# Sliding-window attention and a gated feed-forward block: half 1's attention early in tile 0, tile 0's outputs in tile 1, longer bursts of attention work

## The chip, the core and the metric

The kernel runs on one core of a Trainium2 chip. The core has a matrix engine (TensorE, in the profile PE, with PEld for its weight loads), a vector engine (DVE), a scalar engine (ACT), GpSimd (POOL) and a sync engine (SP) that here only starts transfers. PE writes to PSUM, eight banks of 128 x 512 fp32; DVE and ACT read them. The metric is the time of one execution on the device in microseconds; the median over several runs is compared.

## What is computed

```python
def _attn_ref(q, k, v, n_global, n_local):            # q, k, v: 4 x 8 x 768 x 64
    scores = scale * np.matmul(q, k.transpose(0, 1, 3, 2))
    is_global = pos[None, :] < int(n_global)          # 8
    is_local = (rel >= 0) & (rel < int(n_local))      # 96
    dist = np.where(is_global & ~is_local, float(n_local), np.abs(rel))
    scores = scores - slopes[:, None, None] * dist
    scores = np.where(is_global | is_local, scores, -1e9)
    a = softmax(scores)
    return np.matmul(a, v)

def _moe_ref(x, w_gate, w_val, w_out):                # x: 3072 x 512, ff 1536
    g = x @ w_gate
    return (g * sigmoid(g) * (x @ w_val)) @ w_out
```

The attention's result, heads side by side, is the x of the feed-forward block: 4 batches of 768 tokens, 8 heads of 64, a hidden width of 1536.

## The kernel before

**Tiles.** The 3072 tokens are eight tiles of 384, two to a batch ("half 0" and "half 1" of it). Tile t needs `xT`, the attention's result for its half, transposed, as four chunks of 128 features. Its feed-forward runs over twelve blocks f of 128 hidden units: four matmuls give the gate product (`gps`), four the value product (`vps`), each into one PSUM bank. ACT makes a tanh of the gate (`th`, L513), DVE turns it into x times sigmoid (`sl`, L515) and multiplies the value product by it (`hT`, L519). The banks of these products rotate over x0, x1, x2. An output is 128 tokens by 512; its twelve matmuls come in four parts of three (`out_part`, bank o0), three outputs to a tile; ACT evicts an output after its fourth part and SP stores it.

**Attention.** Heads go in pairs (`Pair`), two pairs to a quad (`Quad`). A pair's scores are taken for seven chunks of keys in three banks' worth of queries, called bk 0, 1 and 2; each head of a pair has a bank of its own out of a0 to a3 (`bank`, `banks`). ACT takes the exponential into `at`; DVE or POOL multiplies by masks that hold the bias and the window. `Quad.values` weighs: a denominator (matmuls with ones) and two numerators into PSUM, ACT copies the numerators (`ns`), DVE inverts the denominator (`invert`) and spreads it over the lanes (`spread`), and two multiplies by `scale_num` give two chunks of `xT`. These are on DVE for batch 0 and on POOL for the others.

**Batches.** Batch 0 is done in a head: half 0 completely before the first feed-forward block, with its bias put in by matmuls (`bias`). Its half 1 (`half1`: `trh` transposes, `sch` scores, `va` values) runs among the blocks of tile 0. Batch 1 is transposed by PE in tile 1 (`first`); batches 2 and 3 are loaded as rows by POOL and transposed by DMA from SP's queue (`fetch`, `transposes_dma`, `turn_ends`) inside the double tiles 2-3 and 4-5 (`both`); `second` is what is left of batch 3, in tile 6.

**Order.** All engines run their instructions in the order in which the program issues them. Six stretches of tiles each have a list of attention steps; a quota, worked out from the sum of work, hands out a step after so many products or output parts (L733 to L760). What follows a burst on ACT and DVE (exponentials of a second pair, masks, inversion, spread, multiplies) goes into a list `later`, of which one item is issued ahead of each product or output part (`run_later(1)`), and all before a further step. Loads have places of their own (`at_step`, L719 to L731), as have the masks (L716 to L718).

**Loads.** POOL starts the loads of q, k, v and the weights, which change fp32 to fp16 on the way (L594 to L612): the weights in pieces of two blocks (`load_w`), half 1 of batch 0 by `load_half(1, ...)`, v in chunks of 120 keys (`load_v_rest`), the output weights by `load_wo`. SP copies the eight global keys and values to their places and stores outputs.

Of the kernel before, what the change touches and what calls it, by code (L numbers as in the profile page):

```python
# [9 lines left out]
FP32 = mybir.dt.float32  # L10
# [6 lines left out]
WIN = 216  # L17
# [20 lines left out]
def kernel(  # L38
# [117 lines left out]
    def stage_rows(b):  # L156
        qst[b] = sb2.tile([128, NP, J, 2, D], FP16, name="qst", tag="qst")
        kst[b] = sb2.tile([128, NP, J, 2, D], FP16, name="kst", tag="kst")
        kend[b] = sb2.tile([128, H, D], FP16, name="kend", tag="kend", bufs=1)
        nc.gpsimd.memset(kend[b], 0.0)  # L160
        nc.sync.dma_start(out=kend[b][0:NG], in_=kG[:, b])
        for hp in range(NP):
            pair = kG[:, b, 2 * hp:2 * hp + 2, :].rearrange("p h d -> p (h d)")
            nc.sync.dma_start(
                out=kst[b][0:NG, hp].rearrange("p t e d -> p t (e d)"),
                in_=pair.unsqueeze(1).broadcast_to([NG, J, 2 * D]))
# [9 lines left out]
    kG = sb.tile([NG, B, H, D], FP16, name="kG")  # L176

    def load_globals():
        for dst, src in ((kG, k), (vG, v)):
            nc.gpsimd.dma_start(  # L180
                out=dst[:, 1:].rearrange("p b h d -> p (b h) d"),
                in_=src[1:, :, 0:NG, :].rearrange("b h p d -> p (b h) d"))
# [55 lines left out]
    def banks(name, dt=FP32):  # L238
        return [bank(name, dt) for _ in range(2)]

# [15 lines left out]
    class Pair:  # L256
# [97 lines left out]
        def scores(self, bk, mul_eng, put_off):  # L354
            hp = self.hp
            sc = banks("sc")
# [45 lines left out]
    class Quad:  # L402
# [33 lines left out]
        def invert(self, den):  # L436
            dT = sb2.tile([128, TB], FP32, name="dT", tag="dT")
            self.dR = sb2.tile([128, TB // 32], FP32, name="dR", tag="dR")
            nc.vector.transpose(dT, den[:, 0:TB])  # L439
            nc.vector.reciprocal(  # L440
                out=self.dR, in_=dT.rearrange("p (n i) -> p n i", i=32)[:, :, 0])
# [10 lines left out]
        def values(self, half, bank, mul_eng):  # L452
# [3 lines left out]
            for side in range(2):  # L456
                num = bank("num")
                self.weigh(half, num, side)
                src = sb2.tile([128, TB], FP32, name="ns", tag="ns")
                nc.scalar.copy(out=src, in_=num[:, 0:TB])  # L460
                srcs.append(src)
# [25 lines left out]

    hTs = {}
# [3 lines left out]
    def products(t, f, which, c0, c1, dst=None):  # L492
        if f == 0 and which == 0 and c0 == 0:
            hTs[t] = sb2.tile([128, NFF, TB], FP16, name="hT", tag="hT", bufs=3)
        if c0 == 0:
            if dst is None:
                dst = single("gv"[which] + "ps", state["x"][gv.get("n", 0) % len(state["x"])])
                gv["n"] = gv.get("n", 0) + 1
            gv[f, which] = dst
# [94 lines left out]
    load_w(0, 2)  # L594
    load_w(2, 4)
    load_w(4, 6)
    load_half(1, 0, 4)
    load_half(1, 4, 8)
    load_w(6, 8)
    load_w(8, 10)  # L600
    for c in range(3, NCH):
        load_v_rest(0, c)
    load_w(10, 12)
    for g in range(3):
        load_wo(g)
    stage(1)
    load_qk(1, 0, 4)
    load_wo(3)
    load_qk(1, 4, 8)
    load_globals()  # L610
# [30 lines left out]
    def sc(b, hp, bk):  # L641
        on_vector = b < 2 or bk < 2 or hp % 2 == 0
        return lambda: pairs[b, hp].scores(bk, nc.vector if on_vector else nc.gpsimd, bool(later))

    def va(b, g, half):
        return lambda: quads[b, g].values(half, bank, nc.vector if b == 0 else nc.gpsimd)
# [4 lines left out]
    def trh(hp):  # L651
        def step():
            pairs[0, hp].transposes_half(1, [t[:, 0:TB] for t in banks("trs", FP16)], V, A)
        return step
# [9 lines left out]
    def second(b):  # L664
        return [[sc(b, 0, 2), sc(b, 1, 2)], [sc(b, 2, 2), sc(b, 3, 2)],
                [va(b, 0, 1)], [va(b, 1, 1)]]

    def fetch(b, *hps):
        def step():
            if hps[0] == 0:  # L670
                turn_ends(b)
            for hp in hps:
                pairs[b, hp].transposes_dma()
        return step

    def first(b):
        return [[tr(b, 0), tr(b, 1)], [sc(b, 0, 0), sc(b, 0, 1)], [tr(b, 2), tr(b, 3)],
                [sc(b, 1, 0), sc(b, 1, 1)], [sc(b, 2, 0), sc(b, 2, 1)], [va(b, 0, 0)],
                [sc(b, 3, 0), sc(b, 3, 1)], [], [va(b, 1, 0)]]

    def both(b):

        n = b + 1

        return [[sc(b, 0, 2), sc(b, 1, 2)], [sc(b, 2, 2), sc(b, 3, 2), fetch(n, 0, 1)],
                [va(b, 0, 1)], [va(b, 1, 1)],
                [sc(n, 0, 0), sc(n, 0, 1), fetch(n, 2, 3)], [sc(n, 1, 0), sc(n, 1, 1)],
                [va(n, 0, 0)], [sc(n, 2, 0), sc(n, 2, 1)],
                [sc(n, 3, 0), sc(n, 3, 1)], [va(n, 1, 0)]]

    half1 = [[trh(0), trh(1)], [trh(2), trh(3)], [sch(0)], [sch(1)],
             [va(0, 0, 1)], [sch(2)], [sch(3)], [va(0, 1, 1)]]

    def ff(t, f0, f1, n_out=(0,)):
# [3 lines left out]
        (ff(0, 0, 4), [], 0, 0),  # L700
        (ff(0, 4, 11) + [(0, 11, 3)], half1, 4.7, 0.4),
        (ff(1, 0, 12, (0, 1, 1, 1)), first(1), 5.0, 0.2),
        (ff(2, 0, 12, (1,)) + ff(3, 0, 12, (1,)), both(1), 6.0, 0.4),
        (ff(4, 0, 12, (1,)) + ff(5, 0, 12, (1,)), both(2), 6.0, 0.4),
        (ff(6, 0, 12, (1,)), second(3), 6.0, 0.4),
        (ff(7, 0, 12, (1,)), [], 0, 0)]

# [8 lines left out]
    for h in range(H):  # L716
        mask_at(0, min(h, 11) if h < 4 else 11, h // 4, h, WIN, 3 * WIN)
        mask_at(h // 4, (8, -4)[h // 4] + h, 0, h, 0, WIN)  # L718
    at_step(1, 1, lambda: [copy_globals(b) for b in range(1, B)])  # L719
    for b, base, rate, v_at in ((2, 19, 2.0, (27, 28, 29, 30, 32, 33, 34)), (3, 43, 1.4, (54, 55, 56, 57, 61, 62, 63))):  # L720
# [13 lines left out]
    for tiles, steps, tail, owed in stretches:  # L734
        groups = []
        for t, f, n_out in tiles:
            groups += [(1.0, t, f, which) for which in range(2)]
            groups += [(1.1, t, f, 2)] * n_out
        work = sum(g[0] for g in groups)
        quota = len(steps) / (work - tail)  # L740
        for w, t, f, which in groups:
            if which == 0:
                for ld in loads.pop((t, f), []):
                    ld()
                if f == 0:
                    run_later(len(later))
            run_later(1)
            if which == 2:
                out_part(*outs.pop(0))
            else:  # L750
                gate_or_val(t, f, which, NC if t == 0 and f < 2 else 0)
                for fn in after.pop((t, f, which), []):
                    fn()
            owed += w * quota
            while owed >= 1.0 and steps:
                run_later(len(later))
                for step in steps.pop(0):
                    step()
                owed -= 1.0
        assert not steps  # L760
# [40 lines left out]
```

The softmax here doesn't subtract the row's maximum and nothing guards it: scores larger than these inputs give would overflow.

## Time and profile before

| | |
|---|---|
| median of 13 runs | 249.35 us (248.46 to 251.6) |
| the profiled execution | 250.95 us, its span 249.2 us |
| PE idle over the span (span less busy) | 9.6 us |
| gate and value products, `gps` and `vps` (L502), 752 matmuls | 77.9 and 77.3 us busy |
| output parts (L531), 276 matmuls | 73.1 us busy |
| DVE `sl` and `hT` (L515, L519), 94 each | 52.0 and 51.9 us busy |
| ACT `th` (L513), 94 | 46.4 us busy |
| ACT exponentials (L373), 72 | 33.2 us busy |
| POOL `xT` multiplies (L464), 24 | 23.9 us busy, 1013 ns each |
| DVE `xT` multiplies (L464), 4 | 2.0 us busy, 548 ns each |
| loads by POOL, rate of all transfers in the first 56 us | 143 to 204 GB/s |

Busy times overlap: PE's matmuls are pipelined, and an entry begins before the one ahead of it has ended. So the distance between starts is the measure of what a matmul costs in a row of others. The idle column of a row of the profile is time of that engine alone; it costs something where the engine is the one that everything waits for.

### The profile page before, as it was taken

Reading aid. Unit: us, or ns where it says so; the run is one execution under the profiler, and the core shown is the slowest. Engines: PE = TensorE matmul, PEld = TensorE weight load, DVE = VectorE, ACT = ScalarE, POOL = GpSimd, SP = SyncE. Lnnn points to the kernel's source line nnn. Section 1 sums busy time; section 2 is a strip of 40 time slices with the busy share of each in tenths; the row PEclk is TensorE's granted clock in tenths of the full one; section 3 lists DMA queues with packets and bytes.
Section 4 is the critical chain, followed back from the end, with each engine's and each line's share of the span. In section 5 each row is a group of like instructions: output and inputs, shape, how many; then the busy total and the mean of one; then the engine's idle time right before and its main releaser. Section 6 shows DMA issues by size and latency. Waiting matters only on the chain.

```text
span 249.2 us, 6076 instructions
## 1 busy us (share of the span) xinstructions
PE 239.6 (96%) x2428; PEld 135.5 (54%) x2428; DVE 159.6 (64%) x346; ACT 130.1 (52%) x289; POOL 116.2 (47%) x139
## 2 busy tenths in 40 slices
PE   6998979999998999999999999999999999999994
PEld 4555545566564555555555555555555555555543
DVE  5668636578885666767775666676766666555510
ACT  5636656787762564564743744555635634332321
POOL 8899986461099934505519777703030232200000
PEclk9999988999999999999999999999999999999999
DMA  8999999999149999941917999951011101100122
GB/s 143 167 171 181 185 173 199 204 162 139 43 36 139 119 159 142 142 73 45 93 45 86 83 158 171 177 74 43 3 42 45 42 3 42 42 10 35 42 85 87
DMA packets 86644, 25.10 MB, mean 101 GB/s; under 512 B 72800, under 2 KB 83672, under 8 KB 86616
## 3 DMA queue, kind: packets, MB, share of 16 engines
q0 software_dynamic: 67472, 14.05, 65.7%
q1 hardware_dynamic: 18584, 10.30, 18.1%
q8 instruction: 19, 0.31, 0.5%
q10 hardware_dynamic: 560, 0.36, 0.5%
q14 instruction: 9, 0.07, 0.1%
HBM read 28.67 MB, written 6.29 MB: 140 GB/s over the span
## 4 chain that ended last, share of the span: by engine, by line
PE 76%; POOL 4%; ACT 1%; issue 1%; DVE 0%; POOLq 0%
PE ops L531 23%; PE gps L502 22%; PE vps L502 21%; PE sc L365 3%; PE num L429 3%; PE den L429 2%; POOL xT L464 1%; POOL qst L193 1%; PE trs L267 1%; PE ops L547 1%; POOL kst L193 1%; ACT at L348 0%; POOL kend L198 0%; DVE sl L515 0%; ACT th L513 0%
## 5 line engine op out<-in xcount | busy, mean ns | idle before, releaser
L515 DVE SCALAR_TENSOR_TENSOR sl<-th,gps 128x384 f32<-128x384 f32 x94 | 52.0, 553 | 52.0 <-ACT th L513 51.3
L513 ACT ACTIVATE th<-gps 128x384 f32<-128x384 f32 x94 | 46.4, 494 | 67.1 <-PE gps L502 65.4
L502 PE MATMUL gps<-xT,wg 128*128 128x384 f16 x376 | 77.9, 328 | 1.3 <-POOL xT L464 1.1
L502 PE MATMUL vps<-xT,wv 128*128 128x384 f16 x376 | 77.3, 328 | 0.7 <-DVE sl L515 0.7
L531 PE MATMUL ops<-wo,hT 128*128 128x512 f16 x276 | 73.1, 379 | 0.0
L519 DVE TENSOR_TENSOR hT<-vps,sl 128x384 f16<-128x384 f32 x94 | 51.9, 552 | 12.1 <-PE vps L502 4.7
L464 POOL TENSOR_TENSOR xT<-ns,rb 128x384 f16<-128x384 f32 x24 | 23.9, 1013 | 72.5 <-DVE rb L445 72.5
L502 PEld LDWEIGHTS <-wg 128*128 128x128 f16 x384 | 36.5, 98 | 33.7 <-issue 2.4
L502 PEld LDWEIGHTS <-wv 128*128 128x128 f16 x384 | 36.3, 98 | 27.2 <-issue 3.6
L531 PEld LDWEIGHTS <-hT 128*128 128x128 f16 x276 | 26.2, 98 | 23.5 <-issue 0.4
L373 ACT ACTIVATE at<-sc 128x432 f16<-128x432 f32 x72 | 33.2, 534 | 9.6 <-PE sc L365 9.6
L170 POOL DMA_DIRECT2D vS<-in_v_dram x28 | 24.8, 899 | 6.5 <-DMA wo<-in_moe_w_out_dram 2.3
L537 ACT ACTIVATE osb<-ops 128x512 f32<-128x512 f32 x23 | 13.7, 597 | 16.7 <-PE ops L531 16.7
L460 ACT COPY ns<-num 128x384 f32<-128x384 f32 x28 | 12.0, 482 | 10.5 <-PE num L429 9.6
L384 DVE TENSOR_TENSOR at<-at,masks 128x864 f16<-128x864 f16 x20 | 12.1, 607 | 7.0 <-ACT at L373 7.0
L193 POOL DMA_DIRECT2D kst<-in_k_dram x16 | 14.1, 889 | 0.0
L429 PE MATMUL num<-at,vS 128*32 128x216 f16 (+6 forms) x560 | 12.3, 226 | 1.7 <-DMA vS<-in_v_dram 1.7
L193 POOL DMA_DIRECT2D qst<-in_q_dram x16 | 13.7, 868 | 0.0
L348 ACT ACTIVATE at<-sc 128x432 f16<-128x432 f32 (+2 forms) x32 | 11.6, 446 | 3.7 <-PE sc L340 3.7
L384 POOL TENSOR_TENSOR at<-at,masks 128x864 f16<-128x864 f16 x4 | 7.3, 1820 | 13.3 <-ACT at L373 13.3
L429 PEld LDWEIGHTS <-vS 128*32 128x32 f16 x560 | 9.7, 95 | 2.3 <-DMA vS<-in_v_dram 2.1
L439 DVE STREAM_TRANSPOSE dT<-den 128x384 f32<-128x384 f32 x16 | 9.3, 578 | 1.6 <-PE den L429 1.6
(71 smaller groups left out, 175.1 us busy)
## 6 DMA issues: line engine op xcount, KB each, us to landing
out_dram<-osb SPq DMA_DIRECT2D x23, 256.0 KB
vS<-in_v_dram POOLq DMA_DIRECT2D x24, 120.0 KB, 6.4
wg<-in_moe_w_gate_dram POOLq DMA_DIRECT2D x12, 128.0 KB, 5.4
wv<-in_moe_w_val_dram POOLq DMA_DIRECT2D x12, 128.0 KB, 5.3
wo<-in_moe_w_out_dram POOLq DMA_DIRECT2D x4, 384.0 KB, 8.6
qst<-in_q_dram POOLq DMA_DIRECT2D x16, 96.0 KB, 3.7
kst<-in_k_dram POOLq DMA_DIRECT2D x16, 90.0 KB, 3.8
kst<-in_k_dram POOLq DMA_DIRECT2D x2, 384.0 KB, 11.2
```

Source lines behind the costliest of these rows:

```text
L170: nc.gpsimd.dma_start(out=vSs[b][NG:NG + n, c, :, :], in_=v[b, :, KC * c:KC * c + n, :].rearrange("h p d -> p h d"))
L193: nc.gpsimd.dma_start(out=st[b][p0:p0 + n, h // 2, :, h % 2, :], in_=src[b, h, 0:n * J].rearrange("(t p) d -> p t d", p=n))
L373: nc.scalar.activation(out=at[:, hi, :], in_=sc[hi][:, 0:BANK], func=AF.Exp, scale=scale)
L384: mul_eng.tensor_mul(at, at, m[:, :, o:o + BANK])
L429: nc.tensor.matmul(dst[r, o:o + n], lhsT=ones[:, 0:32] if side is None else vals[:, 4 * g + j, side::2], rhs=pairs[b, 2 * g + j // 2].at[c ...
L464: mul_eng.tensor_mul(self.x_out(half, side), srcs[side], self.rb)
L502: nc.tensor.matmul(gv[f, which][:, 0:TB], lhsT=w[:, c, 128 * f:128 * f + 128], rhs=x_of(t)[:, c, :], start=(c == 0), stop=(c == NC - 1))
L513: nc.scalar.activation(out=th, in_=dst[:, 0:TB], func=AF.Tanh, scale=0.5)
L515: nc.vector.scalar_tensor_tensor(out=sl, in0=th, scalar=1.0, in1=dst[:, 0:TB], op0=AluOp.add, op1=AluOp.mult)
L519: nc.vector.tensor_mul(hTs[t][:, f, :], dst[:, 0:TB], gv["sl"])
L531: nc.tensor.matmul(ops, lhsT=hTs[t][:, f, 128 * i:128 * i + 128], rhs=wo[:, f, :], start=(f == 0), stop=(f == NFF - 1))
L537: nc.scalar.mul(out=osb, in_=ops, mul=0.5)
```

## The change

It does seven things.

1. Half 1 of batch 0 is loaded between the first weights: heads 0 to 3 after blocks 0 and 1, heads 4 to 7 after blocks 2 and 3. The rest of v comes ahead of the weights of blocks 8 to 11, the global keys and values ahead of the last output weights.
2. `half1` gets written-out places, at the end of blocks 1 to 9 of tile 0; two of its transposes share one bank each.
3. No output part is left in tile 0. Tile 1 has all twelve, five of them in its last block, and the last values of batch 1's half 0 stand between the first and the second of these five.
4. The quota is gone: every step has a tile and a block after which, or an output part before which, it is issued. A step of scores takes two or three pairs; with three, the first of them takes two banks of the rotation x0 to x2 (`spare`).
5. In tiles 2 to 6 both quads of a half are weighed in one step (`both_values`): two denominators into `spare` banks with their inversions at once, then four numerators into a0 to a3. The first quad's multiplies stay on POOL, the second's go to DVE. Batch 1's half 0 is multiplied on DVE too.
6. In the double tiles pairs 0 and 1 of the next batch are scored at block 5 of the first tile, together with the last pair of the batch before; `turn_ends` comes behind the transposes of pairs 2 and 3.
7. Buffers and smaller places: `dT` one buffer, `ns` four; `kG` without the unused batch 0; the masks from block 7 of tile 0 to block 4 of tile 1; `copy_globals` at block 7 of tile 1; loads of batch 2 from block 20 (counted over all tiles), of batch 3 from block 38.

```diff
-    kG = sb.tile([NG, B, H, D], FP16, name="kG")
+    kG = sb.tile([NG, B - 1, H, D], FP16, name="kG")
...
+    def spare(name):
+        tag = state["x"][gv.get("n", 0) % len(state["x"])]
+        gv["n"] = gv.get("n", 0) + 1
+        return single(name, tag)
...
+    def both_values(b, half):
+        two = [quads[b, g] for g in range(2)]
+        for quad in two:
+            den = spare("den")
+            quad.weigh(half, den, None)
+            quad.invert(den)
+        srcs = {}
+        for g, quad in enumerate(two):
+            for side in range(2):
+                num = bank("num")
+                quad.weigh(half, num, side)
+                src = sb2.tile([128, TB], FP32, name="ns", tag="ns", bufs=4)
+                nc.scalar.copy(out=src, in_=num[:, 0:TB])
+                srcs[g, side] = src
...
+        def spread_first():
+            two[0].spread()
+            for side in range(2):
+                scale_num(nc.gpsimd, 0, side)
+
+        later.append(spread_first)
+        later.append(two[1].spread)
+        for side in range(2):
+            later.append(lambda side=side: scale_num(nc.vector, 1, side))
...
     load_w(0, 2)
+    load_half(1, 0, 4)
     load_w(2, 4)
+    load_half(1, 4, 8)
     load_w(4, 6)
-    load_half(1, 0, 4)
-    load_half(1, 4, 8)
     load_w(6, 8)
-    load_w(8, 10)
     for c in range(3, NCH):
         load_v_rest(0, c)
+    load_w(8, 10)
     load_w(10, 12)
-    for g in range(3):
-        load_wo(g)
+    load_wo(0)
+    load_wo(1)
     stage(1)
     load_qk(1, 0, 4)
+    load_globals()
+    load_wo(2)
     load_wo(3)
     load_qk(1, 4, 8)
-    load_globals()
...
+    def sc(b, *units):
+        def step():
+            for i, (hp, bk, *other) in enumerate(units):
+                pair = pairs[b + 1 if other else b, hp]
+                on_vector = pair.b < 2 or bk < 2 or hp % 2 == 0
+                pair.scores(bk, nc.vector if on_vector else nc.gpsimd, bool(later),
+                            [spare("sc") for _ in range(2)] if len(units) == 3 and i == 0
+                            else banks("sc"))
+        return step
...
-        return lambda: quads[b, g].values(half, bank, nc.vector if b == 0 else nc.gpsimd)
+        return lambda: quads[b, g].values(half, bank, nc.vector if b < 2 else nc.gpsimd)
...
     def fetch(b, *hps):
         def step():
-            if hps[0] == 0:
-                turn_ends(b)
             for hp in hps:
                 pairs[b, hp].transposes_dma()
+            if hps[0] > 0:
+                turn_ends(b)
         return step
...
+    def first(t, b):
+        return {(t, 3): [tr(b, 0), tr(b, 1)],
+                (t, 5): [sc(b, (0, 0), (0, 1), (1, 0))],
+                (t, 7): [tr(b, 2), tr(b, 3)],
+                (t, 8): [sc(b, (1, 1), (2, 0), (2, 1))],
+                (t, 9): [va(b, 0, 0)],
+                (t, 10): [sc(b, (3, 0), (3, 1))],
+                (t, 11, 1): [va(b, 1, 0)]}
+
+    def both(t, b):
 
         n = b + 1
...
+        return {(t, 0): [sc(b, (0, 2), (1, 2), (2, 2)), fetch(n, 0, 1)],
+                (t, 5): [sc(b, (3, 2), (0, 0, n), (1, 0, n)), fetch(n, 2, 3)],
+                (t, 8): [vas(b, 1)],
+                (t + 1, 0): [sc(n, (0, 1), (1, 1), (2, 0))],
+                (t + 1, 4): [sc(n, (2, 1), (3, 0), (3, 1))],
+                (t + 1, 8): [vas(n, 0)]}
+
+    def second(t, b):
+        return {(t, 0): [sc(b, (0, 2), (1, 2))], (t, 3): [sc(b, (2, 2), (3, 2))],
+                (t, 7): [vas(b, 1)]}
+
+    half1 = {(0, 1): [trh(0, "o0"), trh(1)], (0, 2): [sch(0)], (0, 3): [sch(1), trh(2), trh(3)],
+             (0, 5): [sch(2)], (0, 6): [va(0, 0, 1)], (0, 7): [sch(3)], (0, 9): [va(0, 1, 1)]}
...
     stretches = [
-        (ff(0, 0, 4), [], 0, 0),
-        (ff(0, 4, 11) + [(0, 11, 3)], half1, 4.7, 0.4),
-        (ff(1, 0, 12, (0, 1, 1, 1)), first(1), 5.0, 0.2),
...
+        (ff(0, 0, 12), half1),
+        (ff(1, 0, 6, (0, 0, 0, 1, 0, 1)) + ff(1, 6, 11, (1,)) + [(1, 11, 5)], first(1, 1)),
...
+    spots = [(0, f) for f in (7, 8, 9, 10, 11, 11)] + [(1, f // 2) for f in range(10)]
+    for n, (t, f) in enumerate(spots):
+        mask_at(t, f, n % 2, n // 2, *((0, WIN), (WIN, 3 * WIN))[n % 2])
+    at_step(1, 7, lambda: [copy_globals(b) for b in range(1, B)])
+    for b, base, rate, v_at in ((2, 20, 2.0, (31, 32, 33, 34, 35, 36, 37)), (3, 38, 1.4, (56, 57, 58, 59, 60, 61, 62))):
...
+    def take(step_list):
+        run_later(len(later))
+        for step in step_list:
+            step()
...
+            for which in range(2):
+                run_later(1)
                 gate_or_val(t, f, which, NC if t == 0 and f < 2 else 0)
...
+            for n in range(n_out):
+                if (t, f, n) in steps:
+                    take(steps.pop((t, f, n)))
+                run_later(1)
+                out_part(*outs.pop(0))
+            if (t, f) in steps:
+                take(steps.pop((t, f)))
```

## The prediction

> **What bounds the kernel now.** I read the engine shares first, then TensorE's waits, then the stretches, then the order of time. TensorE (PE) is busy 96% of the span, so two things can be won: the other 4%, and PE time that is busy without doing dense products.
>
> ```profile
> PE 239.6 (96%) x2428; PEld 135.5 (54%) x2428; DVE 159.6 (64%) x346; ACT 130.1 (52%) x289; POOL 116.2 (47%) x139
> ...
> PEclk9999988999999999999999999999999999999999
> ```
>
> ```profile
> PE num L429 <- DMA vS<-in_v_dram: 1.7, 2, 1.4
> ...
> PE gps L502 <- POOL xT L464: 1.1, 2, 0.6
> ```
>
> ```profile
> 31.20:37.40 6.20, 4.46 (x83) 2.49 (x78) 2.25 (x5) 3.14 (x8) 5.22 (x8) 0.88 1.59 173
> 37.40:43.60 6.20, 6.20 (x60) 3.34 (x58) 3.95 (x8) 4.29 (x12) 3.73 (x6) 0.84 1.25 199
> ...
> 46.10:77.20 31.10, 31.09 (x358) 17.87 (x356) 25.09 (x54) 21.88 (x52) 15.05 (x19) 1.00 1.11 108
> ```
>
> The second fence is PE's waits (us in total, times, longest), the third its stretches: PE, weight load, DVE, ACT and POOL busy us, then PE's clock and the DMA share. The losses sit in tile 0 (about 18.5 to 48 us) and at the start of tile 2 (77 to 79 us). In tile 0 PE waits 1.42 + 0.32 us for values of batch 0, and right after that its clock is halved (the two 8s; 0.88 and 0.84). In tile 1 (third stretch row) PE is full, but DVE is at 25.09 of 31.10 us, which matters below.
>
> From tile 2 on PE streams without a gap, and only its order costs:
>
> ```profile
> 62.27 0.81 PE L531 MATMUL ops<-wo,hT 128*128 128x512 f16 x3
> 63.01 0.54 PE L365 MATMUL sc<-qT,kT 64*128 64x216 f16 x8
> 63.49 0.82 PE L502 MATMUL gps<-xT,wg 128*128 128x384 f16 x4
> ...
> 77.24 0.49 PE L502 MATMUL gps<-xT,wg 128*128 128x384 f16 x2
> 78.16 0.32 PE L502 MATMUL gps<-xT,wg 128*128 128x384 f16 x1 [0.43 <-POOL xT L464]
> 79.10 0.32 PE L502 MATMUL gps<-xT,wg 128*128 128x384 f16 x1 [0.62 <-POOL xT L464]
> 79.26 0.81 PE L502 MATMUL vps<-xT,wv 128*128 128x384 f16 x4
> ```
>
> Starts are what count: a gate or value product (four matmuls) and an output part (three) each take 0.65 us from start to start elsewhere. From the output part at 62.27 to the gate at 63.49 is 1.22 us, so the score burst between costs 0.57 us. Its two pairs stream 2 x 432 columns; at the dense rate (384 columns in 0.1625 us) that is 0.37 us. So **0.21 us of each burst is the changeover** into half-array matmuls and back.
>
> **Part 1: tile 0.** Counting starts from 18.51 us (the first gate not woven into the head), tile 0 holds ten blocks of 1.30 us, four bursts of biased scores of 1.10, two of values of 1.03, and transposes of about 1.5; with 0.1 us of changeover for each of seven bursts that is 21.7 us. Now it ends, less its nine output parts (1.95 us), at 46.3 us: 27.8 us. The 6 us lost are the waits listed for PE there (0.65 + 0.32 + 0.22 + 0.32 + 1.42 + 0.17 = 3.1), 1.65 from the halved clock (four matmuls at 35.98 take 1.25 instead of 0.65, the next four 1.28, the burst at 38.51 1.51 instead of 1.10), and some 1.2 in bank waits inside the transposes.
>
> The new order of loads. POOL's queue lands in order; from the trace's landings a weight piece takes 0.67 us, a half-head piece of k or q 1.03, a chunk of v about 0.95. Weights of blocks 0 and 1 land at 15.1 as now. Then, summing: half 1 heads 0-3 at 17.1, weights 2-3 at 19.8 (now 17.8), heads 4-7 at 22.0, weights 4-5 at 25 (now 21.4), 6-7 at 28, v at 32.6 (now 35.5), weights 8-9 at 35 (now 31), 10-11 at 37.7 as now. In the new order PE wants weights 2-3 at 19.5, 4-5 at 26.5, v at 32, 8-9 at 35.6, 10-11 at 39.5: the moved weights cost nothing, v some 0.2 us. The halved clock goes with the 1.4 us wait.
>
> What is late next is **PSUM banks and DVE**. Walking it: the first scores at block 2 take the bank of the transposes just before, whose six copies on DVE (1.27 us, behind the products of blocks 0 and 1, which end at 20.7) finish at 22.0: 0.55 us. The second transposes wait for exponentials in their bank: 0.3. Delayed gates after bursts (a pair's four exponentials take 1.5 us and hold up the next tanh): 0.6. And the last values are at block 9, two blocks (2.6 us) before tile 1, since the nine output parts that lay between are gone. From the start of that burst to the last xT multiply took 5.5 us before (43.19 to 48.67); one more gate product on DVE (0.55) comes between; PE needs it after 1.13 + 2.6 + 0.49 = 4.2: a **new wait of about 1.6 us at tile 1's start**. Behind it all of tile 1 is queued. Sum: 18.5 + 21.7 + 3.3 = 43.5 against 46.3, **-2.8 us** (bounds -0.8, where DVE binds, and -4.4).
>
> A rule speaks here. The Trainium skill ("TensorE: Matmul & The Clock Gate", "HAM oscillation — how this bites in real kernels") says that the clock is kept as long as no idle gap of PE is over some 3.4 us. By it the new 1.6 us wait costs no clock. The trace disagrees: the gaps before its halved stretch are 0.32 and 1.42 us. By that row such a wait can cost 1.65 more. The old gaps lay among value bursts with hardly a dense product, the new one between dense blocks, so I take 0 and keep +1.7 in the range.
>
> **Part 2: tile 1.** All twelve outputs move here; the count of parts is unchanged, so by tile 2 PE has done the same work. But xT of batch 1's first half goes from POOL to DVE: four multiplies of 0.55 us (the DVE rows of that line) more. DVE's sum in tile 1: twelve blocks at 1.13, transposes' copies 4.5, masks 5.4, two values 5.0 = 28.5 us of some 31. The densest part, from the second transposes (block 7) to block 11, has 12.7 us of DVE in 11.7 us of PE. I take **+1.2 us** of waits (bounds 0.2 and 2.5; only gate and value banks two products ahead cover it). The ten masks now in blocks 0 to 4 are 0.8 us of ACT per block, beside tanh at 0.4 in 1.3: covered, barely.
>
> **Part 3: tile 2's start.** 77.24 to 79.26 is 2.02 us where 0.65 is due: 1.37 lost to POOL's multiplies (1.0 us each, behind DMA issues). Now the burst stands before four output parts: PE arrives 1.0 + 2.6 + 0.4 = 4.0 us after its start, the chain (denominator 0.45, inversion and spread 1.4, two DVE multiplies 1.0, hand-overs) takes 3.2. **-1.37**.
>
> **Part 4: bursts.** Outside tile 0, five score bursts fewer (two in each of the double tiles, one in tile 1) at 0.21: -1.05. Five value bursts fewer, each saving between the 0.09 us gap ahead and 0.21: 0.15, -0.75. **-1.8**.
> The price of merging: the first of three pairs takes two gate banks. Its second matmul waits for the gate product just made (`sl`), with the whole PE queue behind it. Over the blocks of the trace `sl` ends 1.28 us after its gate (1.39 in the worst tenth); PE arrives after a value product, an output part and the changeover, 1.45. Covered; uncovered it costs up to 0.5 a burst. The exponentials of pairs two and three fall where no output is evicted (parts end at blocks 3, 7, 11). After a burst of two quads DVE has two inversions, two spreads and two multiplies (about 3.8 us) and the gate after next ends some 0.1 late: 5 x 0.1 = **+0.5**.
>
> **Moved at no cost:** key globals without batch 0 and the single `dT` buffer (same engine, in order); `copy_globals` from block 1 to 7 (its keys land near 46, its values are used past 60 us); POOL loads of batch 2, no longer stuck behind xT (POOL idles until 69.0 now), so they land before tile 2; `turn_ends` behind the pair transposes, as SP issues them in order and `kE` is first used in the next double tile.
>
> **Sum:** -2.8 + 1.2 - 1.37 - 1.8 + 0.5 = -4.3 us. The profiled execution took 250.95 us (span 249.2 and 1.75 around it): **246.6 us**. It lies 1.6 above the median, 249.35; the runs fall into two groups, 248.5 to 249.4 and 250.4 to 251.6. Should the halved clock be what parts them, which one trace can't show, a median run has less to win, so against the median the change is some 2.7 us.
>
> **Rivals.**
> A, the forecast, 246.6 (245 to 248.2): chance 0.54.
> B, **DVE becomes the bound** in tiles 0 and 1: tile 0 wins 0.8 only and tile 1 loses 2.5. For it: 81% DVE in tile 1 now, and the sums above. Against: DVE waits for tanh before nearly each gate product in tile 0 now. 250.95 - 0.8 - 1.37 - 1.8 + 2.5 + 0.5 = 250.0: chance 0.2.
> C, banks and the tile 1 start hide everything: no boundary wait (-1.5) and no waits in tile 1 (-1.2): 243.9, chance 0.13.
> D, **slower: transposes by DMA.** Pairs 0 and 1 of the next batch are turned behind the burst at block 0 and now used at block 5: 0.7 + 5 x 1.95 = 10.5 us later, where the trace has 20.0 (issued at 82.33, first used at 102.34). In the trace the first four ran until about 93.9, 11.6 us, beside POOL loads; the last four (from 152.46) took 7.4 with little beside them. With the loads gone from that place I take 7.4, no wait. It decides from 10.5 us on; at 13 us, and a halved clock behind each of the two waits, it costs 2 x (2.5 + 1.7) = 8.4: 255; at 11.6 with the clock, 2 x 2.8: 252. Chance 0.13.
>
> **Range and chances.** The range runs from 243.8 (C) to 250.3 (B) and leaves D and a little out; A alone has 245 to 248.2. Faster by over 0.5% (what this measurement can tell from nothing), below 248.1: A and C, 0.66. Between 248.1 and 250.6: most of B, 0.2. Slower: D and the rest of B, 0.14.
>
> **What would show it.** In the new profile: no 8 in PEclk and no wait for v over 0.5 us (part 1); a PE wait for DVE's xT at tile 1's start of about 1.6 us, with tile 1 starting near 42; no wait for POOL's xT at tile 2; triple score bursts about 0.75 us from end of block to next gate; no wait for `sl` inside a burst. Wrong would be: PE waiting for `kT` or `qT` at block 5 of tiles 2 and 4 (D), DVE near full until 75 us (B), or a halved clock in a new place.

## The result, and the profile after

The changed kernel takes 246.56 us in the median of 11 runs (246.16 to 248.87), the kernel before 249.63 us beside it (48 runs, 247.51 to 251.6). The medians lie 3.07 us, or 1.2%, apart. The ratio of the means is 0.990, its 95% interval 0.987 to 0.993, so the changed kernel is faster by 1.0%; it leaves out five slow runs of the kernel before, those over 1.5% above its fastest. The profiled execution took 246.26 us, its span 244.5 us, where that of before took 250.95 and 249.2.

The engine shares and the clock on the page of the changed kernel:

```profile
PE 235.6 (96%) x2428; PEld 136.1 (56%) x2428; DVE 166.9 (68%) x360; ACT 128.9 (53%) x289; POOL 102.2 (42%) x125
...
PEclk9999999999999999999999999999999999999999
```

Its waits of PE (us in total, times, longest):

```profile
PE sc L334 <- ACT qT L325: 1.2, 1, 1.2
PE vps L533 <- DVE sl L546: 0.9, 2, 0.5
PE den L433 <- DVE at L385: 0.8, 1, 0.8
PE gps L533 <- DVE xT L468: 0.6, 1, 0.6
```

And its stretches (PE, weight load, DVE, ACT, POOL, then clock and DMA), two over the same times as in the prediction and the whole of tile 1:

```profile
31.20:37.40 6.20, 6.20 (x102) 3.89 (x101) 4.25 (x9) 4.88 (x14) 6.20 (x9) 1.00 1.18 153
37.40:43.60 6.20, 5.75 (x87) 3.28 (x85) 5.05 (x11) 4.33 (x11) 3.21 (x5) 1.00 1.23 185
43.80:75.70 31.90, 30.53 (x352) 17.75 (x352) 26.91 (x57) 22.39 (x52) 23.58 (x28) 1.00 1.97 159
```

PE's share is still 96%: the row of shares doesn't show that anything has changed. What has changed stands in the other two views. The waits for v and for POOL's `xT` are gone, the clock is full, and in their place are four waits for ACT and DVE, all before 73 us. Three of them are seen in PE's order of time:

```profile
20.56 0.58 PE L334 MATMUL sc<-dist,slopeI 128*128 128x72 f16 x5
22.31 0.34 PE L334 MATMUL sc<-dist,slopeI 128*128 128x432 f16 x1 [1.17 <-ACT qT L325]
...
42.94 0.78 PE L533 MATMUL gps<-xT,wg 128*128 128x384 f16 x3
44.34 0.32 PE L533 MATMUL gps<-xT,wg 128*128 128x384 f16 x1 [0.61 <-DVE xT L468]
...
71.17 0.43 PE L433 MATMUL den<-at,ones 128*32 128x216 f16 x10
72.38 0.48 PE L433 MATMUL den<-at,ones 128*32 128x144 f16 x6 [0.78 <-DVE at L385]
```

The first two lines are the scores at block 2 of tile 0. The next two are tile 1's first gate, whose third and fourth chunk of `xT` are late. The last two are the last values of tile 1. Tile 2's first gate follows without a gap (the gate starts at 75.94 and the value product at 76.58), and no wait of PE is listed after it. A burst of three pairs:

```profile
87.75 0.81 PE L562 MATMUL ops<-wo,hT 128*128 128x512 f16 x3
88.50 0.73 PE L369 MATMUL sc<-qT,kT 64*128 64x216 f16 x14
89.16 0.82 PE L533 MATMUL gps<-xT,wg 128*128 128x384 f16 x4
```

From the output part's start to the gate's start 1.41 us, less 0.65 for the part: 0.76 us for three pairs, where two took 0.57.

**Where the time went**, from the starts in both traces. A tile's begin is taken as the start of its first value product less 0.65 us, so that a wait inside its first gate counts to the tile before; the nine matmuls of output that the kernel before had in tile 0 are counted to tile 1 in both.

| | before | after | difference |
|---|---|---|---|
| up to tile 1 | 46.28 us | 43.85 us | -2.43 us |
| tile 1, with tile 2's start | 32.33 us | 32.09 us | -0.24 us |
| tile 2 to the end | 170.57 us | 168.55 us | -2.02 us |

Together -4.69, the difference of the profiled times. Of the first row 0.26 us lie in the head, whose first woven product starts at 15.06 instead of 15.32.

### The profile page after: what moved, and what is told of

The parts are those of the page before. It is cut to its first block, busy times and chain, and to the rows that moved or that the text cites. A ratio compares the mean times of both kernels' runs of the same rounds, so it can differ in the third digit from the quotient of the medians.

```text
span 244.5 us, 6058 instructions
## 1 busy us (share of the span) xinstructions
PE 235.6 (96%) x2428; PEld 136.1 (56%) x2428; DVE 166.9 (68%) x360; ACT 128.9 (53%) x289; POOL 102.2 (42%) x125
## 4 chain that ended last, share of the span: by engine, by line
PE 82%; POOL 5%; DVE 5%; DMA 4%; ACT 2%; issue 1%; DVEq 0%; POOLq 0%
PE ops L562 24%; PE gps L533 23%; PE vps L533 23%; PE sc L369 3%; PE num L433 3%; DMA vS<-in_v_dram 3%; PE den L433 2%; DMA wg<-in_moe_w_gate_dram 2%; DVE sl L546 1%; POOL wv L212 1%; POOL wg L212 1%; POOL q L118 1%; PE trs L272 1%; PE ops L578 1%; POOL k L118 1%
## 5 line engine op out<-in xcount | busy, mean ns | idle before, releaser
L533 PE MATMUL gps<-xT,wg 128*128 128x384 f16 x376 | 77.1, 327 | 0.7 <-DVE xT L468 0.6
L533 PE MATMUL vps<-xT,wv 128*128 128x384 f16 x376 | 76.4, 326 | 0.9 <-DVE sl L546 0.9
L533 PEld LDWEIGHTS <-wv 128*128 128x128 f16 x384 | 37.5, 98 | 27.5 <-issue 2.9
L533 PEld LDWEIGHTS <-wg 128*128 128x128 f16 x384 | 35.1, 98 | 31.1 <-issue 2.1
L562 PEld LDWEIGHTS <-hT 128*128 128x128 f16 x276 | 26.9, 98 | 23.9
L508 POOL TENSOR_TENSOR xT<-ns,rb 128x384 f16<-128x384 f32 x10 | 9.8, 994 | 65.5 <-DVE rb L449 54.5
L504 ACT COPY ns<-num 128x384 f32<-128x384 f32 x20 | 8.1, 493 | 7.9 <-PE num L433 7.9
L433 PE MATMUL num<-at,vS 128*32 128x216 f16 (+6 forms) x560 | 11.2, 226 | 0.0
L385 DVE TENSOR_TENSOR at<-at,masks 128x432 f16<-128x432 f16 x24 | 8.1, 378 | 4.1 <-ACT at L377 4.1
```

The source lines that it names most:

```text
L433: nc.tensor.matmul(dst[r, o:o + n], lhsT=ones[:, 0:32] if side is None else vals[:, 4 * g + j, side::2], rhs=pairs[b, 2 * g + j // 2].at[c ...
L533: nc.tensor.matmul(gv[f, which][:, 0:TB], lhsT=w[:, c, 128 * f:128 * f + 128], rhs=x_of(t)[:, c, :], start=(c == 0), stop=(c == NC - 1))
L562: nc.tensor.matmul(ops, lhsT=hTs[t][:, f, 128 * i:128 * i + 128], rhs=wo[:, f, :], start=(f == 0), stop=(f == NFF - 1))
```

## The experiments

Medians are set against the changed kernel's; each ratio is to the kernel before, timed in the same series, with its interval. The unaltered changed kernel was timed once more beside the last of them.

> The changed kernel itself, unaltered, beside the former on the same chip: 246.6 us, granted clock 1.0 in most executions.

246.42 us, ratio 0.988 (0.984 to 0.991). With the 246.56 above that makes 246.5 us, and the differences below are to this. The kernel before had medians of 249.18, 249.61 and 249.23 us beside the three series, and banks, filler, relief and the three together have four runs each. So a difference of some tenths between medians can be the series' and not the edit's; there the traces decide.

**v late.**

```diff
+    load_w(8, 10)
+    load_wo(0)
     for c in range(3, NCH):
         load_v_rest(0, c)
-    load_w(8, 10)
     load_w(10, 12)
-    load_wo(0)
     load_wo(1)
```

> The changed kernel, with the rest of v loaded behind the weights of blocks 8 and 9 and the first output weights, so that it lands near 35.3 us as it did before the change. My theory: the values at block 6 (PE arrives near 32.7) wait about 2.3 us for v, as they waited 1.7 us before, and nothing later gives that back: +2.3 us on the changed kernel's 246.6, and in part of the executions the clock is halved for 3.4 us behind it (granted clock 0.993 instead of 1.0), another +1.7. Rival: the wait for v is hidden by later waits of tile 0 (for sl at block 9, for xT at tile 1's start), so less than +1 us and no change of the clock.

250.69 us, ratio 1.006 (1.003 to 1.008): 4.2 us slower than with v early. PE in order of time, then the stretch behind the wait:

```profile
33.86 0.28 PE L433 MATMUL num<-at,vS 128*32 128x216 f16 x4 [0.71 <-DMA vS<-in_v_dram]
34.59 0.26 PE L433 MATMUL num<-at,vS 128*32 128x168 f16 x4 [0.45 <-DMA vS<-in_v_dram]
35.44 0.81 PE L433 MATMUL num<-at,vS 128*32 128x48 f16 x24 [0.59 <-DMA vS<-in_v_dram]
36.18 1.46 PE L533 MATMUL gps<-xT,wg 128*128 128x384 f16 x4
37.44 1.49 PE L533 MATMUL vps<-xT,wv 128*128 128x384 f16 x4
```

```profile
35.40:38.80 3.40, 3.36 (x34) 1.82 (x35) 0.59 (x2) 1.72 (x4) 3.40 (x6) 0.50 1.31 200
```

The values take 3.77 us (32.41 to 36.18) instead of 1.03, +2.74. Then the clock is at 0.50, a product starts 1.26 to 1.28 us after the one before it instead of 0.65, and about 1.3 us more are lost. Nothing later gives any of it back: the profiled execution is 4.06 us longer than that of the changed kernel. In 17 of 20 executions the mean granted clock was below 0.996 (median 251.2 us; the three others 249.6). So the rival, that later waits hide the one for v, falls.

**xT on POOL.**

```diff
-        return lambda: quads[b, g].values(half, bank, nc.vector if b < 2 else nc.gpsimd)
+        return lambda: quads[b, g].values(half, bank, nc.vector if b == 0 else nc.gpsimd)
```

> The changed kernel with batch 1's xT multiplied on POOL as before. My theory: a wait for POOL's xT of 1.0 to 1.4 us is back at the start of tile 2, and DVE, rid of two multiplies among blocks 10 and 11 of tile 1, shortens the wait of the last values for their mask (0.8 us now, 1.2 with what surrounds it) by about 0.6: +0.4 to +0.8 us. Rival: DVE is what bounds tile 1, then the kernel gets no slower, or faster by up to 1 us. Second rival: the place of the last values alone took away the wait at tile 2 (four output parts behind them), then no wait for POOL's xT and up to -0.6.

250.43 us, ratio 1.004 (1.002 to 1.006): +3.9 us, several times what was expected, and not for the reason expected. There is no wait for POOL's `xT` at tile 2 (its first gate starts at 76.08, the value product at 76.80): as the second rival has it, the four output parts behind the last values cover POOL as well. The time is lost here, in the burst at block 5 of tile 2:

```profile
88.71 0.55 PE L369 MATMUL sc<-qT,kT 64*128 64x216 f16 x10
91.65 0.36 PE L369 MATMUL sc<-qT,kT 64*128 64x216 f16 x4 [2.39 <-DMA qT<-qst]
```

POOL stood before `xT` until 69.6 us, with the last rows of q and k of batch 2 behind it, and v behind these:

```profile
69.58 2.33 POOL L468 TENSOR_TENSOR xT<-ns,rb 128x384 f16<-128x384 f32 x2 [6.69 <-DVE rb L449]
...
81.69 1.70 POOL L193 DMA_DIRECT2D qst<-in_q_dram  x2
83.35 2.79 POOL L170 DMA_DIRECT2D vS<-in_v_dram  x3
```

In the changed kernel the same loads have no `xT` ahead of them:

```profile
70.08 1.77 POOL L193 DMA_DIRECT2D qst<-in_q_dram  x2
71.74 2.85 POOL L170 DMA_DIRECT2D vS<-in_v_dram  x3
98.04 1.95 POOL L508 TENSOR_TENSOR xT<-ns,rb 128x384 f16<-128x384 f32 x2 [23.45 <-DVE rb L449]
```

So in this run the transposes by DMA, issued from SP from 78.6 to 84.7 us, run beside these loads. In the changed kernel POOL loads nothing at that time. PE gets the fourth of them at 91.65, 13.1 us after the first was issued (78.56), and was ready for it at 89.26, 10.7 us after. In the changed kernel their last packet ends 6.5 us after the first issue (78.35 to 84.9). This is the prediction's rival D, for one of its two waits. The change has it covered by letting DVE multiply `xT`, at a small price: the last values of tile 1 take 2.16 us in the changed kernel and 1.89 here. The profiled execution, at full clock, is 2.9 us longer than that of the changed kernel; in 14 of the 20 executions the clock was below 0.996, and their median is 1.1 us above that of the other six.

**Short bursts.** Tiles 2 to 6 in bursts of two pairs and one quad:

```diff
-        return {(t, 0): [sc(b, (0, 2), (1, 2), (2, 2)), fetch(n, 0, 1)],
-                (t, 5): [sc(b, (3, 2), (0, 0, n), (1, 0, n)), fetch(n, 2, 3)],
-                (t, 8): [vas(b, 1)],
...
+        return {(t, 0): [sc(b, (0, 2), (1, 2)), fetch(n, 0, 1)],
+                (t, 2): [sc(b, (2, 2), (3, 2))],
+                (t, 5): [sc(n, (0, 0), (1, 0)), fetch(n, 2, 3)],
+                (t, 8): [va2(b, 0, 1)],
+                (t, 9): [va2(b, 1, 1)],
...
```

> The changed kernel with tiles 2 to 6 in bursts of two pairs and of one quad, in places next to the present ones, engines as now: nine bursts more. My theory: 9 x 0.21 us of changeover, +1.9 us, PE streaming without gaps otherwise. Rival: merged bursts cost as much in bank waits as they save, then within 0.5 us of the changed kernel.

248.43 us, ratio 0.997 (0.995 to 0.999): +1.9 us, as worked out, and without a wait in tiles 2 to 6. One of its bursts:

```profile
88.19 0.81 PE L562 MATMUL ops<-wo,hT 128*128 128x512 f16 x3
88.93 0.55 PE L369 MATMUL sc<-qT,kT 64*128 64x216 f16 x8
89.41 0.82 PE L533 MATMUL gps<-xT,wg 128*128 128x384 f16 x4
```

1.22 less 0.65 us, 0.57 for two pairs; three take 0.76. So a pair costs 0.19 us and a burst 0.19 to 0.2 besides.

**Loads alone**, in the kernel before:

```diff
     load_w(0, 2)
+    load_half(1, 0, 4)
     load_w(2, 4)
+    load_half(1, 4, 8)
     load_w(4, 6)
-    load_half(1, 0, 4)
-    load_half(1, 4, 8)
     load_w(6, 8)
-    load_w(8, 10)
     for c in range(3, NCH):
         load_v_rest(0, c)
+    load_w(8, 10)
```

> The kernel before with only the order of the first loads changed (half 1 among the first weights, v ahead of blocks 8 to 11), its steps where they were. My theory: order and places belong together. The 1.7 us of waits for v and the halved clock (1.65 in the profiled execution) go, but PE now reaches blocks 2 and 4 before their weights: waits for weights of about 1 us and 1.5 to 2 us. Sum -0.6 us on the kernel before (-1.6 to +0.4). Rival: the load order alone carries tile 0's gain, then -2.4 us or better.

249.53 us, ratio 1.0005 (0.998 to 1.003): no change. The waits for v are gone, and the weights of blocks 2 and 4 are waited for:

```profile
19.50 0.50 PE L502 MATMUL gps<-xT,wg 128*128 128x384 f16 x2 [0.47 <-DMA wg<-in_moe_w_gate_dram]
...
23.77 0.50 PE L502 MATMUL gps<-xT,wg 128*128 128x384 f16 x2 [0.85 <-DMA wg<-in_moe_w_gate_dram]
```

Its profiled execution (248.36 us) is the fastest of its twenty, so only the median is compared. So the order of loads is worth nothing without the new places of the steps. The converse, the new places with the whole old order, was not run; the v-late run has them with v alone late, and loses. As the clock was full in 66 of 71 runs of the kernel before, the halved clock that the theory counted on removing was not in the median either.

**Banks.** Three edits to the transposes of half 1 in tile 0: the first pair's k and q get a bank each; the second pair's still share one, but ACT makes all its copies; the third pair uses o0.

```diff
-    def trh(hp, tag=None):
+    def trh(hp, tag=None, k_tag=None, k_eng=V):
         def step():
             t = single("trs", tag, FP16) if tag else bank("trs", FP16)
-            pairs[0, hp].transposes_half(1, [t[:, 0:TB], t[:, TB:2 * TB]], V, A)
+            tk = single("trs", k_tag, FP16) if k_tag else t
+            pairs[0, hp].transposes_half(1, [t[:, 0:TB], tk[:, TB:2 * TB]], k_eng, A)
...
-    half1 = {(0, 1): [trh(0, "o0"), trh(1)], (0, 2): [sch(0)], (0, 3): [sch(1), trh(2), trh(3)],
+    half1 = {(0, 1): [trh(0, "o0", "x2"), trh(1, k_eng=A)], (0, 2): [sch(0)], (0, 3): [sch(1), trh(2, "o0"), trh(3)],
```

> The changed kernel with half 1's transposes in tile 0 off the shared banks: the first pair's k and q in two banks, the second pair's copies both on ACT, the third pair in o0. My theory: the 1.17 us wait of the scores at block 2 stands because ACT copies q only after DVE has copied k out of the same bank; it goes, and 0.3 us at the second transposes too: -1.5 us on the changed kernel's 246.6, that is 245.1, with everything behind it earlier by that. Rival: weights (blocks 4 and 5 at 24.0 to 24.7 us) or the DVE chain at tile 1's start take up what is freed, then less than 0.5 us.

245.11 us, ratio 0.982 (0.978 to 0.986): -1.4 us. What stood in the way is read from ACT's and DVE's order of time in the changed kernel:

```profile
21.19 1.07 ACT L325 COPY qT<-trs 128x384 f16<-128x384 f16 x2 [2.57 <-DVE kT L311]
```

```profile
20.42 1.27 DVE L311 COPY kT<-trs 128x96 f16<-128x96 f16 x6
```

ACT was idle for 2.57 us with q transposed since 19: its copies came only behind those of k, which lay in the same bank, and DVE came to these at 20.42. In the kernel before, with k and q in banks of their own, ACT did not wait for DVE (ACT's copies from 23.89, DVE's from 24.44):

```profile
23.89 0.86 ACT L320 COPY qT<-trs 128x384 f16<-128x384 f16 x2 [0.62 <-PE trs L293]
```

The sixth matmul of the scores takes the bank of the second pair, which ACT's copies leave at 22.26. In the banks run ACT copies the first pair's q at 19.68, ahead of DVE's k (21.19), and is through with the second pair at 21.09; the scores at block 2 run through:

```profile
21.31 0.76 PE L334 MATMUL sc<-dist,slopeI 128*128 128x72 f16 x6
22.00 0.47 PE L345 MATMUL sc<-qT,kT 64*128 64x72 f16 x10
22.41 0.82 PE L533 MATMUL gps<-xT,wg 128*128 128x384 f16 x4
```

1.10 us instead of 2.43. The run does not tell what each of the three edits is worth, nor do the traces tell whether the chip or only the program's order makes the second reader of a bank wait. Here the whole kernel starts its first woven product 0.8 us later than in the changed kernel's profile (15.83 against 15.06), ahead of anything that the edit touches; from there to the end of the span it is 1.7 us shorter (227.7 against 229.4).

**Filler.** Two output parts of tile 0 back in its last block:

```diff
-        (ff(0, 0, 12), half1),
-        (ff(1, 0, 6, (0, 0, 0, 1, 0, 1)) + ff(1, 6, 11, (1,)) + [(1, 11, 5)], first(1, 1)),
+        (ff(0, 0, 11) + [(0, 11, 2)], half1),
+        (ff(1, 0, 6, (0,)) + ff(1, 6, 11, (1,)) + [(1, 11, 5)], first(1, 1)),
```

> The changed kernel with the first two output parts of tile 0 back in tile 0's last block (in tile 1, blocks 3 and 5 lose theirs). My theory: 1.3 us of PE work goes where PE waits 1.3 us for xT at tile 1's start: -1.3 us, 245.3, if blocks 0 to 5 of tile 1 have no waits without them. Rival: DVE bounds the first half of tile 1, which needs these parts as cover, and the 1.3 us come back there: within 0.3 us of the changed kernel.

246.07 us, ratio 0.986 (0.982 to 0.989): -0.4 us, a third of what was expected. The wait at tile 1's start is gone: from the last value product of tile 0 to the first of tile 1 it is 2.49 us in the changed kernel, 1.19 more than the 1.30 of two products, and here 2.60 with the two output parts between, which is just the 2.60 of four. But the burst of three pairs at block 5 now has no output part ahead of it:

```profile
53.56 0.26 PE L369 MATMUL sc<-qT,kT 64*128 64x216 f16 x1
54.00 0.71 PE L369 MATMUL sc<-qT,kT 64*128 64x216 f16 x11 [0.17 <-DVE sl L546]
54.66 0.81 PE L533 MATMUL gps<-xT,wg 128*128 128x384 f16 x4
```

Its second matmul stands 0.44 us in the gate's bank until `sl` is done: 1.10 us from start to next start instead of 0.66. The prediction had put up to 0.5 on a burst whose cover is gone. From the first woven product to the end of the span this run is 0.7 us shorter (228.76 against 229.43).

**Relief.** The last scores of tile 1 a block earlier, one pair of those before taken out to block 6, and the first values a block later:

```diff
+                (t, 6): [sc(b, (1, 1))],
                 (t, 7): [tr(b, 2), tr(b, 3)],
-                (t, 8): [sc(b, (1, 1), (2, 0), (2, 1))],
-                (t, 9): [va(b, 0, 0)],
-                (t, 10): [sc(b, (3, 0), (3, 1))],
+                (t, 8): [sc(b, (2, 0), (2, 1))],
+                (t, 9): [sc(b, (3, 0), (3, 1))],
+                (t, 10): [va(b, 0, 0)],
```

> The changed kernel with batch 1's last scores of half 0 one block earlier, one pair taken out to block 6, and the first values one block later. My theory: the 1.2 us wait of tile 1's last values stands because the last pair's exponentials and masks are issued behind tanh and hT of block 11; with two blocks between them it goes, for one more changeover (0.21): -1.0 us, 245.6. Rival: DVE as a whole bounds tile 1 (28.5 of 31 us); then the wait moves to tile 2's first gate (wait for DVE's xT) and less than 0.3 us is won.

245.8 us, ratio 0.984 (0.980 to 0.988): -0.7 us. In the changed kernel the masks that the last values wait for stand behind `hT` on DVE:

```profile
71.47 0.56 DVE L550 TENSOR_TENSOR hT<-vps,sl 128x384 f16<-128x384 f32 x1
71.95 0.67 DVE L385 TENSOR_TENSOR at<-at,masks 128x432 f16<-128x432 f16 x2
```

PE in the relief run at the last values and tile 2's start, then the same stretch of tile 1:

```profile
72.21 0.45 PE L433 MATMUL den<-at,ones 128*32 128x216 f16 x16
72.50 0.70 PE L433 MATMUL num<-at,vS 128*32 128x216 f16 x32
73.13 2.76 PE L562 MATMUL ops<-wo,hT 128*128 128x512 f16 x12
75.73 1.10 PE L533 MATMUL gps<-xT,wg 128*128 128x384 f16 x4
```

```profile
44.60:76.50 31.90, 31.32 (x356) 17.93 (x356) 26.81 (x56) 23.10 (x53) 23.63 (x28) 1.00 1.91 159
```

The values take 0.92 instead of 2.16 us, although DVE has the same work in the tile (26.81 us against 26.91). A small part (0.29 us) comes back at tile 2's gate (75.73 to 76.67), where DVE's `xT` is late. So both theories had a share, and the order of the instructions had about three quarters of it.

**All three, and then with cover.**

> The three together. My theory: they are independent, -3.8 us, 242.8; granted clock 1.0. Rival: with PE 3 us earlier the loads are late (q and k of heads 4 to 7 of batch 1 land at 56.6, wanted then near 56; output weights at 42.1), and 1 us or more of it is lost to waits for them.

244.19 us, ratio 0.979 (0.974 to 0.984): -2.3 us. No wait for the late loads that the rival named. The expected -3.8 was the sum of three expectations; the medians of the three single runs sum to -2.5. The profiled execution (245.77 us) is the slowest of the four: it lost time in the head, where the clock was halved as well, and starts its first woven product at 17.58, 2.5 us later than the changed kernel. From there to the end of the span it takes 226.4 us against 229.4, -3.0, and the three single traces give -1.7, -0.7 and -0.7 in the same way. So the three gains add up; the filler's is smaller than expected, for the burst without cover.

In the last version that burst doesn't use gate banks:

```diff
-                (t, 5): [sc(b, (0, 0), (0, 1), (1, 0))],
-                (t, 6): [sc(b, (1, 1))],
+                (t, 5): [sc(b, (0, 0), (0, 1))],
+                (t, 6): [sc(b, (1, 0), (1, 1))],
```

> The three edits together, with tile 1's first scores as two bursts of two pairs (blocks 5 and 6) in place of three and one, so that no pair sits in a gate bank where no output part stands ahead of the burst. My theory: the 0.44 us that the burst at block 5 lost to its wait for sl (1.10 instead of 0.66) goes, the count of bursts stays: -0.4 us on the three together (244.2), 243.8. Rival: DVE is behind there anyway and the wait moves to the next product, no change.

243.59 us, ratio 0.976 (0.972 to 0.981), 2.8 us below the unaltered changed kernel beside it (246.42): the fastest version. Its burst at block 5 takes 0.48 us without a wait. Against the three together the gain is not clear of noise: 0.6 us in the medians of two series, 0.2 us in the traces from the first woven product on.

## Why the prediction was right, and where its steps were off

The forecast was 246.6 us, the median is 246.56. The profiled execution moved by -4.7 us where the sum has -4.3; so the terms can be gone through one by one. That the time agrees to 0.04 us is in part luck: tile 0 gained 0.4 us less than its term and the part from tile 2 on 0.9 more, and the sum was set on a profiled execution 1.3 us above the median of its kernel.

**Tile 0: -2.8 forecast, -2.4 measured.** v lands before it is wanted and the clock stays full; the v-late run shows that both belong to v. In the walk, the wait at block 2 was taken at 0.55 us and is 1.3 with what surrounds it: that the transposes' banks would be late was right, but the prediction counted only DVE's copies, and ACT's came behind them. The delayed gates cost 1.2 us from start to start (0.52 and 0.33 of it idle) where 0.6 was taken, the wait for v nothing where 0.2 was, tile 1's start 1.2 where 1.6 was. One word was wrong: the prediction calls what left the last block "nine output parts"; it is three parts, nine matmuls, and the 1.95 us stand for these.

**Tile 1: +1.2 forecast, +1.24 measured, for another reason in the main.** The prediction let DVE's whole load bind, 28.5 us of some 31; it was 26.9 of 31.9. PE is full in the tile but for one wait, of the last values for a mask. The exponentials of the last pair are issued behind the tanh of block 11 and its mask behind `hT`; the relief run takes the wait away with DVE as loaded as it was. The size agreed by luck; the step's mechanism was for the most part another.

**Tile 2's start: -1.37 forecast, gone as forecast.** But the prediction gave it to DVE and the place of the values together. The run with `xT` on POOL shows that the place alone does it. DVE is needed for the loads that POOL would else hold back.

**Bursts: -1.8 forecast outside tile 0, and +0.5 given back; -2.0 measured from tile 2 on.** The short bursts cost 1.9 us for nine in tiles 2 to 6, so the value bursts save about the full 0.2 too, not 0.15. The 0.5 us for DVE behind two quads did not come at all: behind each of the five such bursts PE's products start 0.65 us apart, within 0.01 us. That the gate banks are free in time holds wherever an output part stands ahead of the burst, and fails by 0.44 us where none does, as the filler run shows.

**The median.** The prediction left open whether the halved clock parts the two groups of runs before. It doesn't: among 71 executions of the kernel before beside the first experiments, 5 have a clock below 0.996, and those at full clock alone run from 248.0 to 251.1 us. So the profiled execution was one of few with the loss of 1.65 us (the five have a median 1.7 us above the others'), and a median run had about that much less to win: -4.7 in the profile, -3.1 in the medians. What spreads the runs at full clock stays open. The note that the change is some 2.7 us against the median was nearer than its reason.

**Rivals.** B (DVE as the bound) is refuted by the relief run for most of tile 1. C did not happen, as both its waits are there. D did not happen either, but the run with `xT` on POOL brought one of its two waits about, at about the point that was named (10.5 us). The readings behind D were not alike: 11.6 us runs from the first issue, 7.4 from the first packet. From first issue to last packet the four from 152.46 took about 8.9 us, with loads beside them, and in the changed kernel, with none, 6.5.

## What to carry to other kernels

Where one engine is near full, sum starts and not busy times: a changeover between full-array products and short matmuls cost 0.2 us of PE that no row shows as idle, and merging bursts pays it fewer times, as long as the banks that the longer burst takes are covered by other work. A wait for an engine need not be that engine's load; at block 2 and at the last values of tile 1 it was mostly its order. Look at what was issued ahead of the late instruction, and at whether two engines share a bank, before moving work elsewhere. And a load that is moved earlier is worth what the consumer's new place makes of it; here the new order of loads alone gave nothing.

## What the runs showed that was not expected

PE's clock was halved for about 3.4 us behind gaps well below that length. In the kernel before they were 0.32 and 1.42 us (clock 0.50 from 36.0 to 39.3), in the v-late run 0.71, 0.45 and 0.59, with value bursts between them. In the profiled execution of the three edits together they were 0.53 and 0.67 us in the head, among transposes and short scores:

```profile
9.18 0.36 PE L298 MATMUL trs<-ident,k 128*64 128x128 f16 x6 [0.53 <-DMA k<-in_k_dram]
10.21 0.36 PE L298 MATMUL trs<-ident,q 128*64 128x128 f16 x6 [0.67 <-DMA q<-in_q_dram]
```

```profile
11.00:14.40 3.40, 3.40 (x47) 1.77 (x44) 1.50 (x6) 1.95 (x6) 2.79 (x5) 0.50 1.49 180
```

But the single gap of 2.39 us in the run with `xT` on POOL, with dense products on both sides of its scores, left the clock of the profiled execution full, here in the 3.41 us behind it:

```profile
91.65:95.06 3.41, 3.41 (x23) 1.91 (x24) 1.27 (x3) 2.26 (x6) 0.00 (x0) 1.00 1.62 153
```

Where the clock of that run's 14 executions below 0.996 was lowered, no trace shows. The waits at block 2 and at tile 1's start left it full in all but 2 of the 11 timed runs of the changed kernel, as the prediction had judged. The rule that the prediction weighed, no gap over some 3.4 us, is too mild for these traces, and the length of a gap alone does not order them. That the work around a gap counts fits all of these traces, but no run varied it on its own.

The new order also steadied the kernel: executions at full clock spread over 3.1 us before (66 runs), and nine of the eleven after lie within 1.6 us, the twenty with short bursts within 0.9. The order of loads alone is not what does it: its 17 runs at full clock spread over 2.3 us. What else steadied it was not tried on its own.
